# Copying A's rows 0 to 63 into T from SyncE's queue instead of ScalarE's, in a fused attention and feed-forward kernel

## The chip, the core and the metric

The kernel runs on one core of a Trainium2 chip. A core has five engines that run side by side, each in the order of its own instruction list: TensorE (PE) multiplies matrices, VectorE (DVE), ScalarE (ACT) and GpSimd (POOL) do elementwise work and reductions, and SyncE (SP) only issues DMAs. DMAs are issued from SyncE's queue or from ScalarE's. The metric is the device time of one execution in microseconds, the median of several runs.

## The reference

There are 4 batches of 8 heads with 768 positions of 64 features, and 16 centroids for each head.

```python
q_assign = argmax(q_n @ c_n.T); k_assign = argmax(k_n @ c_n.T)      # normalized q, k, centroids
scores = where(q_assign == k_assign, q @ k.T / 8, -1e9)
attn = exp(scores - max); attn = attn / (sum + 1e-9)
x = (attn @ v) with the heads side by side                            # 3072 x 512
h = x @ w_in                                                          # 512 -> 2048
out = (h * tanh(log1p(exp(h)))) @ w_out                               # 2048 -> 512
```

All inputs and the output are float32. Q and k of a head arrive stacked, 128 partitions by 768.

## The kernel before

**Precision.** Values are split into a high and a low part, and a product is made of three (high by high, high by low, low by high). For the scores of head n, A holds the high parts of q (partitions 0 to 63) and k (64 to 127), scaled; B holds the low parts. `prep_hi` on POOL makes A (lines 484 and 487), `prep_lo` on POOL makes B (line 500). T gets A's rows 0 to 63, Z gets B's rows 64 to 127, and then B's upper rows are overwritten from T and A's lower rows from A's upper rows: `copy_t`, `copy_z`, `copy_b`, `copy_a`. A cluster code (`hot_copy`) fills rows 64 to 79 of T and Z, so that one product adds the mask. The scores of a tile are two pairs of matmuls, B by A and T by Z (lines 631 and 636).

**Units.** The 32 heads n are cut into three units each of 256 query rows, 96 units i = 3n + qb, with two tiles a of 128 rows. The first 24 units (batch 0) run in float32: `rowmax` (VectorE), `expo` (ScalarE), transposes of p on TensorE, copies `pt` by ScalarE and VectorE, `pv`. Beside them the weights are loaded and split (`w_abs`, `w_low`, `w_f32`, `w_sq`, `w_hi`, `w_lo`; `w_lo` on VectorE is line 347). From unit 24 on, the probabilities are split into `hl` by `p_hi` (POOL, line 700) and `p_lo` (VectorE, line 717), and `ptrans` turns them by a DMA from SyncE's queue (`pt<-hl`, line 733). `pv` (line 753) multiplies a pair of units at once and needs all four transposes of the pair. `pv_out` (ScalarE) and `x_lo` (VectorE, line 814) make x; `m1`, `e_mish`, `e_gh`, `e_gl` and `m2` are the feed-forward part, which runs between the units of the next batch. A tail after the last unit uses seven products in place of eight.

**Order.** Every step has a due time in units of i, from the tables T and N, plus an entry of SHIFT for single steps. `Plan.run` issues the steps in the order of the due times, each after the steps that it needs, and ties the instructions of each engine to that order. So the tables fix the order on every engine and in every queue; the data set when an instruction can start. For n ≥ 9 the due time of a copy is 3n + N[kind]. A copy to T exists as a DMA for the 30 heads n ≥ 2; for the first two heads ScalarE copies.

**Queues.** `queue(n, kind)` chooses the issuing queue from T["dq", kind]: an integer other than 0 gives ScalarE, 0 gives SyncE. Before, `copy_t` has 3 and `copy_b` has −9 (both ScalarE); `copy_z` and `copy_a` have 0 (SyncE; most of `copy_a` is computed on ScalarE). The loads of qk, v and the weights, all transposes and the stores go out on SyncE's queue. T and Z have two buffers each, so the copy for n has to wait until the scores of n − 2 are done.

Of the kernel before, what the change touches and what calls it, by code (L numbers as in the profile page):

```python
# [72 lines left out]
def tile_clustered_attention_mish_ffn(  # L73
# [1211 lines left out]
    'v_sqd': -4.311,  # L1285
    'cent_put': -17.026,
    'ffn': 23.993,
    'w_f': 0.36,
    'w_q': 0.842,
    'w_lo': 0.312,  # L1290
    ('z', 'prep_hi'): -17.145,
    ('z', 'prep_lo'): -10.644,
    ('z', 'copy_t'): -21.55,
    ('z', 'copy_a'): -16.804,
    ('z', 'copy_b'): -16.943,
    ('z', 'copy_z'): -16.451,
# [31 lines left out]
    'copy_t': -0.79,  # L1328
    'prep_lo': -0.348,
    'prep_hi': 12.289,  # L1330
    'load': -4.71,
# [10 lines left out]
    ('dq', 'copy_t'): 3,  # L1342
# [25 lines left out]
    ('q_lo', 1): 6.955,  # L1368
# [25 lines left out]
    ('w_s', 1): -0.008,
# [41 lines left out]
    'pv': [4.606, 11.977, 4.089],
    'pv_out': 7.569,
    'x_lo': 2.785,
    'm1': [0.153, 0.664, 1.179, 1.534],
    'e_mish': [11.931, 1.622],  # L1440
    'e_gh': [2.313, 2.115],
    'e_gl': [1.659, 2.92],
# [10 lines left out]
    ('expo', 11, 0): -0.001, ('w_load', 10): -0.351, ('pv_out', 18): -0.443, ('scores', 24, 1): -0.221,  # L1453
    ('copy_b', 8): 0.081, ('scores', 25, 1): -1.54, ('w_lo', 2): 0.002, ('p_lo', 26, 1): 3.011,
    ('scores', 6, 0): -0.211, ('recip', 29, 0): 0.006, ('assign_mm', 0): 5.035, ('qk_load', 0): -4.812,
    ('qk_load', 1): 0.018, ('qk_load', 2): -7.858, ('qk_load', 3): 0.077, ('w_f32', 29): 3.258, ('w_low', 18): 0.746,
    ('w_low', 22): -0.606, ('pv', 5, 0): 0.121, ('w_low', 19): -0.124, ('pv_out', 10): 6.683,
# [12 lines left out]
    ('rowmax', 5, 0): 0.009, ('v_load', 1, 3): 0.118, ('w_load', 6): 0.644, ('copy_z', 0): -0.211,  # L1470
    ('prep_lo', 6): 5.99, ('copy_a', 6): -0.475, ('hot_copy', 0): 3.185, ('p_lo', 9, 1): 1.655,
    ('scores', 6, 1): 0.161, ('ptrans', 6, 0): 0.01, ('w_low', 4): 8.668, ('w_f32', 30): -0.084,
    ('w_f32', 28): -0.139, ('w_f32', 31): 0.04, ('copy_a', 7): 0.131, ('copy_a', 10): 0.5, ('p_hi', 13, 0): 1.089,
    ('p_hi', 14, 0): -3.366, ('p_hi', 15, 0): 0.165, ('p_hi', 16, 0): -3.157, ('p_hi', 16, 1): 0.035,
# [5 lines left out]
    ('copy_t', 0): 2.283, ('v_high', 0, 2): 1.174, ('assign_back', 2): -0.02, ('rowmax', 15, 0): -0.209,  # L1480
    ('x_lo', 16): 1.557, ('total', 19, 0): 0.011, ('assign_turn', 0): 0.477, ('hot_copy', 1): -0.189,
    ('pv_out', 12): 0.25, ('w_f32', 22): 0.284, ('pv_out', 23): 0.18, ('prep_lo', 9): -0.611, ('w_lo', 6): 0.291,
    ('x_lo', 27): 0.772, ('e_gh', 4): 1.076, ('assign_mm', 2): -0.078, ('hot_copy', 7): 0.903, ('hot_copy', 8): 0.259,
    ('p_lo', 14, 1): -0.992, ('p_lo', 2, 0): 0.919, ('scores', 0, 0): 2.293, ('expo', 3, 1): -0.54,
# [604 lines left out]
```

## Time and profile before

| what | us |
|---|---|
| median of 3 runs | 863.29 |
| lowest and highest | 861.83, 864.39 |
| the profiled execution, its own time | 866.38 |
| its span, first to last instruction | 864.6 |
| granted TensorE clock, mean | 1.0 |
| busy: TensorE, VectorE, ScalarE, POOL | 838.4, 690.2, 517.5, 431.4 |

The profile is of one execution. A busy time is the union of an engine's instructions; the issuing of DMAs is not counted as busy, and all of SyncE's work is of that kind. Matmuls are pipelined, so a busy TensorE is not one at its peak.

### The profile page before, as it was taken

Reading aid. Unit: us, or ns where it says so; the run is one execution under the profiler, and the core shown is the slowest. Engines: PE = TensorE matmul, PEld = TensorE weight load, DVE = VectorE, ACT = ScalarE, POOL = GpSimd, SP = SyncE. Lnnn points to the kernel's source line nnn. Section 1 sums busy time; section 2 is a strip of 40 time slices with the busy share of each in tenths; the row PEclk is TensorE's granted clock in tenths of the full one; section 3 lists DMA queues with packets and bytes.
Section 4 is the critical chain, followed back from the end, with each engine's and each line's share of the span. In section 5 each row is a group of like instructions: output and inputs, shape, how many; then the busy total and the mean of one; then the engine's idle time right before and its main releaser. Section 6 shows DMA issues by size and latency. Waiting matters only on the chain.

```text
span 864.6 us, 17394 instructions
## 1 busy us (share of the span) xinstructions
PE 838.4 (97%) x6671; PEld 613.0 (71%) x6671; DVE 690.2 (80%) x1178; ACT 517.5 (60%) x878; POOL 431.4 (50%) x410
## 2 busy tenths in 40 slices
PE   7999899989999999999999999999999999999998
PEld 3676676767777777776776766776777776777787
DVE  7989999898988798788877798777978876488831
ACT  6868878766565766565465765564564665245520
POOL 1464665686467446556576556465566543110000
PEclk9999999999999999999999999999999999999999
DMA  9865572398789987898889976988788876000000
GB/s 347 254 177 157 172 203 76 71 189 169 135 154 194 189 155 134 159 187 148 143 183 179 171 156 117 181 155 145 127 161 140 138 140 123 13 1 14 1 31 32
DMA packets 253060, 121.51 MB, mean 141 GB/s; under 512 B 230288, under 2 KB 230800, under 8 KB 252976
## 3 DMA queue, kind: packets, MB, share of 16 engines
q1 hardware_dynamic: 247632, 108.46, 60.7%
q10 hardware_dynamic: 5344, 11.93, 6.5%
q8 instruction: 53, 0.87, 0.5%
q14 instruction: 31, 0.25, 0.1%
HBM read 35.72 MB, written 6.29 MB: 49 GB/s over the span
## 4 chain that ended last, share of the span: by engine, by line
PE 73%; DVE 13%; DMA 6%; ACT 3%; issue 2%; POOL 2%; ACTq 0%; SPq 0%; DVEq 0%; POOLq 0%
PE o L753 9%; PE h L832 8%; PE h L834 8%; PE h L833 8%; PE O L873 7%; PE O L875 7%; PE O L874 7%; PE s L631 5%; PE s L636 5%; DVE m L648 4%; DMA pt<-hl 4%; DVE hl L717 2%; PE as L543 1%; DMA stage<-in_w_out_dram 1%; DVE w L347 1%
## 5 line engine op out<-in xcount | busy, mean ns | idle before, releaser
L662 ACT ACTIVATE p<-s,m 128x768 f32<-128x768 f32 x192 | 172.6, 899 | 159.4 <-DVE m L648 110.0
L700 POOL TENSOR_SCALAR hl<-p,l 128x768 f16<-128x768 f32 x144 | 167.4, 1165 | 171.9 <-DVE l L682 77.3
L648 DVE TENSOR_REDUCE m<-s 128x1 f32<-128x768 f32 x192 | 181.4, 950 | 26.7 <-PE s L636 24.5
L717 DVE SCALAR_TENSOR_TENSOR hl<-p,l,hl 128x768 f16<-128x768 f32 x144 | 172.2, 1200 | 11.8 <-POOL hl L700 11.3
L832 PE MATMUL h<-x,w 128*128 128x256 f16 x640 | 175.6, 274 | 1.4 <-DVE pt L729 0.7
L833 PE MATMUL h<-x,w 128*128 128x256 f16 x640 | 174.4, 273 | 0.0
L834 PE MATMUL h<-x,w 128*128 128x256 f16 x640 | 174.4, 273 | 0.0
L873 PE MATMUL O<-w,g 128*128 128x512 f16 x320 | 121.7, 380 | 0.0
L874 PE MATMUL O<-w,g 128*128 128x512 f16 x320 | 121.3, 379 | 0.0
L875 PE MATMUL O<-w,g 128*128 128x512 f16 x320 | 121.3, 379 | 0.0
L631 PE MATMUL s<-A,B 128*128 128x384 f32 x384 | 117.3, 386 | 2.6 <-ACT p L662 2.5
L849 POOL TENSOR_SCALAR g<-u,mscg 128x512 f16<-128x512 f32 x80 | 77.3, 969 | 66.3 <-ACT u L843 56.8
L857 DVE SCALAR_TENSOR_TENSOR g<-u,mscg,g 128x512 f16<-128x512 f32 x80 | 82.9, 1037 | 24.4 <-POOL g L849 24.2
L636 PE MATMUL s<-Z,T 80*128 80x384 f32 x384 | 99.2, 339 | 1.0 <-DVE T L603 1.0
L832 PEld LDWEIGHTS <-w 128*128 128x128 f16 x768 | 75.1, 98 | 28.6 <-issue 17.6
L753 PE MATMUL o<-pt,v 128*64 128x256 f16 x1296 | 79.4, 274 | 5.8 <-DMA pt<-hl 5.8
L833 PEld LDWEIGHTS <-w 128*128 128x128 f16 x768 | 75.5, 98 | 12.5 <-issue 1.5
L834 PEld LDWEIGHTS <-w 128*128 128x128 f16 x768 | 75.1, 98 | 8.7
L753 PEld LDWEIGHTS <-v 128*64 128x64 f16 x1296 | 68.6, 110 | 16.2 <-issue 9.9
L631 PEld LDWEIGHTS s<-A,B 128*128 128x128 f32 x384 | 62.2, 190 | 16.4 <-issue 4.6
L636 PEld LDWEIGHTS s<-Z,T 80*128 80x128 f32 x384 | 69.8, 189 | 1.3 <-ACT Z L600 1.3
L843 ACT ACTIVATE u<-h,msch 128x512 f32<-128x512 f32 x80 | 52.2, 686 | 29.0 <-PE h L834 21.9
(225 smaller groups left out, 1301.3 us busy)
## 6 DMA issues: line engine op xcount, KB each, us to landing
qk<-in_qk_dram SPq DMA_DIRECT2D x32, 384.0 KB, 4.7
stage<-in_w_in_dram SPq DMA_DIRECT2D x16, 512.0 KB, 7.4
stage<-in_w_out_dram SPq DMA_DIRECT2D x16, 512.0 KB, 4.5
vraw<-in_vP_dram SPq DMA_DIRECT2D x16, 384.0 KB, 5.7
T<-A ACTq DMA_DIRECT2D x30, 192.0 KB, 3.2
Z<-B SPq DMA_DIRECT2D x30, 192.0 KB, 3.4
B<-T ACTq DMA_DIRECT2D x28, 192.0 KB, 3.2
out_dram<-osb SPq DMA_DIRECT2D x20, 256.0 KB, 2.3
```

The lines of the kernel that those rows point to most:

```text
L631: nc.tensor.matmul(s[:, j, :384], st["B", n][:, q0 : q0 + P], st["A", n][:, j * 384 : (j + 1) * 384], start=True, stop=False,)
L636: nc.tensor.matmul(s[:, j, :384], st["T", n][: D + NCL, q0 : q0 + P], st["Z", n][: D + NCL, j * 384 : (j + 1) * 384], start=False, stop=True,)
L648: nc.vector.tensor_reduce(m, st["s", i, a][:, :, :384], axis=AX.XY, op=ALU.max, negate=True)
L662: nc.scalar.activation(p.rearrange("p (n x) -> p n x", n=2), st["s", i, a][:, :, :384], AF.Exp, bias=st["m", i, a], scale=1.0, accum_out=l,)
L717: nc.vector.scalar_tensor_tensor(t[:, 1], p, r, t[:, 0], op0=ALU.mult, op1=ALU.subtract)
L753: nc.tensor.matmul(o[s * D : s * D + D, :256], v if early else v[:, int(part == 1)], st["pt", 2 * m + s][:, :, c + (0 if early or part < 2 ...
L832: nc.tensor.matmul(o, wh, xh, start=(c == 0), stop=False)
L833: nc.tensor.matmul(o, wh, xl, start=False, stop=False)
L834: nc.tensor.matmul(o, wl, xh, start=False, stop=(c == 3))
L873: nc.tensor.matmul(o, gh, wh, start=(f == 0 and fi == 0), stop=False)
L874: nc.tensor.matmul(o, gh, wl, start=False, stop=False)
L875: nc.tensor.matmul(o, gl, wh, start=False, stop=(f == 7 and fi == 1))
```

## The change

The integer for `copy_t` in T becomes 0, so that its 30 DMAs go out on SyncE's queue. The function bodies stay as they are. The rest of the diff is new values in T, N and SHIFT: 54 of T's 129 entries, 37 of N's 48, and in SHIFT 1502 changed, 357 new and 4 dropped of 2524. Its core, with the entries that the prediction speaks of:

```diff
@@ T
-    ('dq', 'copy_t'): 3,
+    ('dq', 'copy_t'): 0,
-    'copy_t': -0.79,
+    'copy_t': -0.776,
-    'w_lo': 0.312,
+    'w_lo': 0.316,
...
@@ N
     'prep_hi': -3.459,
-    'copy_t': -2.7,
+    'copy_t': -3.354,
     'copy_z': -2.222,
-    'copy_a': -1.917,
+    'copy_a': -1.909,
...
@@ SHIFT
-    ('copy_t', 5): -0.446,
+    ('copy_t', 5): 0.094,
-    ('copy_t', 22): 0.405,
+    ('copy_t', 22): 1.078,
-    ('rowmax', 78, 1): 0.01,
+    ('rowmax', 78, 1): -0.277,
-    ('x_lo', 74): 0.255,
+    ('x_lo', 74): 0.338,
+    ('x_lo', 75): 0.968,
+    ('w_lo', 15): 3.882,
...
```

The due times of the single steps named below follow from these values and the formulas of the listing; `w_lo(15)`, for one, is due at N["ws"][15] + T["w_lo"] + SHIFT, 25.018 + 0.312 before and 24.953 + 0.316 + 3.882 now.

## Rows read from the trace of the kernel before

**Rows 1.** The page, part 1: busy time, share of the span, instructions.
```profile
PE 838.4 (97%) x6671; PEld 613.0 (71%) x6671; DVE 690.2 (80%) x1178; ACT 517.5 (60%) x878; POOL 431.4 (50%) x410
```

**Rows 2.** Windows: stretch, length, busy PE, PEld, DVE, ACT, POOL, clock, DMA, GB/s.
```profile
60.00:120.00 60.00, 54.78 (x434) 40.14 (x432) 57.72 (x97) 49.52 (x93) 32.67 (x39) 1.00 0.63 185
120.00:180.00 60.00, 54.84 (x421) 41.17 (x419) 53.33 (x101) 43.77 (x84) 40.79 (x41) 1.00 0.42 93
180.00:740.00 560.00, 553.90 (x4466) 401.39 (x4465) 457.24 (x758) 332.15 (x541) 327.48 (x286) 1.00 0.84 156
```

**Rows 3.** Waits of TensorE: total us, times, longest.
```profile
PE o L753 <- DMA pt<-hl: 5.8, 6, 1.6
```

**Rows 4.** Instructions on tile A: DMA issues, duration ns min/median/max.
```profile
L514 ACTq DMA_DIRECT2D T<-A x30: 468/468/518, 30.8 to 681.6; - x30
...
L514 SPq DMA_DIRECT2D A<-A x7: 494/536/1382, 74.8 to 673.7; - x7
```

**Rows 5.** The chain that ended last, 60 to 130 us: start, us, what.
```profile
88.54 0.47 ACTq L514
```

**Rows 6.** Timeline of TensorE, seven waits; the idle time before is in brackets.
```profile
89.58 1.08 PE L753 MATMUL o<-pt,vraw 128*64 128x256 f32 x6 [0.41 <-ACT pt L731]
...
111.44 0.76 PE L710 MATMUL q<-ident,p 128*128 128x128 f32 x5 [0.58 <-ACT p L662]
...
170.37 0.27 PE L832 MATMUL h<-x,w 128*128 128x256 f16 x1 [0.70 <-ACT u L843]
...
175.92 0.61 PE L631 MATMUL s<-A,B 128*128 128x384 f32 x2 [2.04 <-ACT p L662]
...
182.71 1.50 PE L753 MATMUL o<-pt,v 128*64 128x256 f16 x24 [0.96 <-DMA pt<-hl]
...
464.50 1.17 PE L753 MATMUL o<-pt,v 128*64 128x256 f16 x18 [1.38 <-DMA pt<-hl]
...
594.87 2.15 PE L753 MATMUL o<-pt,v 128*64 128x256 f16 x35 [1.62 <-DMA pt<-hl]
```

**Rows 7.** Timeline of ScalarE, two places.
```profile
108.91 0.47 ACTq L514 DMA_DIRECT2D T<-A  x1
...
461.10 0.47 ACTq L514 DMA_DIRECT2D T<-A  x1
```

**Rows 8.** DMA issues, 180 to 740 us: count, KB each, median us to landing.
```profile
Z<-B SPq DMA_DIRECT2D x22, 192.0 KB, 3.6
T<-A ACTq DMA_DIRECT2D x21, 192.0 KB, 3.3
...
pt<-hl SPq DMA_TRANSPOSE x140, 4.1
```

**Rows 9.** The chain before the pairs 60 and 76.
```profile
458.84 5.62 DMA pt<-hl
...
582.25 0.36 ACTq L514
...
583.75 0.42 DVE xx L814
...
587.74 0.87 DVE m L648
...
589.22 5.60 DMA pt<-hl
```

**Rows 10.** Timeline of SyncE, 455 to 470 us.
```profile
460.65 0.89 SPq L474 DMA_DIRECT2D qk<-in_qk_dram  x1
461.60 0.44 SPq L356 DMA_DIRECT2D vraw<-in_vP_dram  x1
```

**Rows 11.** Waits of SyncE's queue: total us, times, longest.
```profile
SPq L733 <- DVE hl L717: 133.4, 56, 5.3
```

**Rows 12.** Timeline of VectorE and of POOL at 167 us.
```profile
167.13 1.42 DVE L347 SCALAR_TENSOR_TENSOR w<-w,ws1r,w 128x1024 f16<-128x1024 f32 x1
...
167.46 1.87 POOL L700 TENSOR_SCALAR hl<-p,l 128x768 f16<-128x768 f32 x1
```

More of the change, by code (lines that the diff above doesn't have):

```diff
@@ L1427 @@
     'E': [0.384, 0.793, 1.234, 1.538],
-    'scores': 1.991,
+    'scores': 1.774,
     'rowmax': -0.3,
-    'expo': 3.904,
-    'total': 6.224,
+    'expo': 10.884,
+    'total': 6.302,
     'recip': 0.225,
-    'p_hi': 13.925,
-    'p_lo': 5.917,
+    'p_hi': 9.06,
+    'p_lo': 5.07,
     'ptrans': 0.818,
[L1436 to L1442, printed above, removed]
@@ L1449 @@
+    'm_out': 9.793,
+    'm_store': -0.442,
[3 rows of a table added]
 }
 SHIFT = {
[L1453 to L1457, printed above, removed]
@@ L1470 @@
[L1470 to L1474, printed above, removed]
@@ L1480 @@
[L1480 to L1484, printed above, removed]
@@ L1579 @@
-    ('p_hi', 24, 1): 0.826, ('p_hi', 25, 1): 0.716, ('p_lo', 28, 0): 0.229, ('p_lo', 28, 1): 2.539,
-    ('v_split', 0, 3): -0.06, ('v_split', 0, 1): -0.016, ('v_load', 1, 1): 0.317, ('ptrans', 19, 1): 0.105,
-    ('scores', 17, 1): 0.001, ('x_lo', 13): 0.266, ('p_hi', 9, 0): -0.021, ('pv_out', 19): 0.371,
-    ('pv_out', 17): 0.019, ('w_hi', 9): 4.053, ('w_low', 16): -0.221, ('w_lo', 3): 0.014, ('assign_hot', 2): 0.072,
-    ('rowmax', 22, 1): -0.123, ('expo', 15, 0): -0.084, ('qk_load', 7): 0.323, ('w_abs', 22): -0.017,
@@ L1584 @@
-    ('copy_a', 2): -1.413, ('m1', 6, 0): 1.422, ('e_gl', 1): -0.009, ('assign_back', 0): 2.408, ('w_abs', 20): -0.927,
-    ('pv_out', 8): 0.554, ('scores', 16, 0): 2.317, ('rowmax', 31, 0): -0.143, ('w_abs', 4): 0.104,
-    ('assign_max', 0): 1.285, ('hot_copy', 6): 0.017, ('assign_back', 1): 0.088, ('ptrans', 17, 1): -0.007,
-    ('expo', 6, 1): 1.076, ('x_lo', 29): -0.101, ('scores', 15, 0): 0.598, ('w_hi', 14): 0.913, ('copy_z', 8): 0.487,
-    ('p_lo', 17, 0): 0.344, ('scores', 1, 1): 3.429, ('rowmax', 19, 1): 0.01, ('w_sq', 16): 1.215,
@@ new lines @@
+    ('x_lo', 16): 1.557, ('total', 19, 0): 0.474, ('assign_turn', 0): 0.604, ('hot_copy', 1): -0.189,
+    ('pv_out', 12): 0.357, ('w_f32', 22): 0.369, ('pv_out', 23): 2.957, ('prep_lo', 9): -0.629, ('w_lo', 6): 0.291,
+    ('x_lo', 27): 0.592, ('e_gh', 4): 1.076, ('assign_mm', 2): 0.08, ('hot_copy', 7): 0.903, ('hot_copy', 8): 0.554,
+    ('p_lo', 14, 1): -0.992, ('p_lo', 2, 0): 1.367, ('scores', 0, 0): 2.293, ('expo', 3, 1): -0.54,
+    ('ptrans', 29, 0): 0.146, ('w_sum', 1): -0.11, ('assign_put', 2): 0.408, ('w_abs', 6): 0.161,
@@ new lines @@
+    ('w_load', 3): -0.316, ('rowmax', 26, 1): -0.136, ('total', 17, 1): -0.068, ('expo', 23, 0): -0.177,
+    ('w_lo', 10): -0.61, ('pv_out', 15): 0.265, ('assign_mm', 3): 3.259, ('p_lo', 12, 1): -0.197,
+    ('total', 20, 1): 1.896, ('e_gh', 2): -0.268, ('w_sq', 27): 3.267, ('w_sq', 6): 2.585, ('copy_b', 0): 0.86,
+    ('scores', 4, 0): 0.259, ('w_hi', 1): 0.386, ('hot_copy', 11): 0.649, ('prep_hi', 0): -0.295, ('w_load', 8): 2.33,
+    ('ptrans', 26, 1): -0.021, ('prep_hi', 3): -6.754, ('hot_copy', 3): -0.631, ('w_sq', 18): 0.052,
@@ new lines @@
+    ('scores', 25, 0): 0.563, ('scores', 26, 0): -0.169, ('ptrans', 24, 1): 0.073, ('ptrans', 25, 1): 0.037,
+    ('ptrans', 26, 0): 0.002, ('ptrans', 27, 0): -0.072, ('ptrans', 27, 1): -0.023, ('ptrans', 28, 1): -0.023,
+    ('ptrans', 29, 1): 0.054, ('prep_lo', 1): 0.695, ('x_lo', 22): 5.096, ('copy_z', 2): -0.303, ('w_load', 31): 0.66,
+    ('recip', 12, 1): 0.994, ('copy_a', 11): 0.022, ('total', 0, 0): 3.405, ('w_load', 2): -0.292,
+    ('total', 3, 1): 0.367, ('w_low', 20): 0.225, ('rowmax', 19, 0): 0.245, ('assign_stg', 0): -14.81,
@@ new lines @@
+    ('ptrans', 7, 1): 0.028, ('pv_out', 21): 1.094, ('p_lo', 27, 1): 1.452, ('recip', 26, 0): -0.024,
+    ('w_abs', 29): 0.05, ('total', 1, 0): -0.471, ('w_low', 0): 0.153, ('w_low', 2): -0.261, ('w_low', 7): 3.585,
+    ('w_low', 5): -0.999, ('w_low', 8): -1.486, ('w_low', 10): -0.254, ('copy_z', 11): 0.051, ('w_sq', 5): 0.304,
+    ('expo', 21, 0): -0.373, ('p_hi', 8, 1): -0.044, ('rowmax', 25, 1): 0.005, ('prep_hi', 11): 1.306,
+    ('m1', 2, 1): -0.458, ('hot_copy', 4): 4.62, ('w_abs', 12): -0.053, ('pv_out', 7): -0.005, ('w_sq', 3): 0.003,
@@ new lines @@
+    ('hot_copy', 6): 0.017, ('assign_back', 1): 0.105, ('ptrans', 17, 1): -0.15, ('expo', 6, 1): 0.969,
+    ('x_lo', 29): -0.101, ('scores', 15, 0): 0.569, ('w_hi', 14): 1.124, ('copy_z', 8): 0.487, ('p_lo', 17, 0): 0.344,
+    ('scores', 1, 1): 3.486, ('rowmax', 19, 1): 0.01, ('w_sq', 16): 1.215, ('w_abs', 14): -0.403,
+    ('recip', 4, 0): -1.418, ('expo', 5, 1): -0.85, ('w_lo', 0): -0.058, ('assign_put', 0): -2.449,
+    ('total', 0, 1): -0.188, ('total', 16, 1): 4.336, ('v_high', 0, 0): 3.268, ('scores', 10, 1): 0.05,
@@ new lines @@
+    ('x_lo', 5): 13.019, ('w_sq', 19): 6.549, ('qk_load', 8): -0.024, ('w_load', 1): 0.431, ('recip', 16, 1): 1.328,
+    ('expo', 12, 1): 2.798, ('x_lo', 14): -0.015, ('ptrans', 18, 0): -0.016, ('m1', 4, 1): -0.446, ('w_hi', 4): 0.039,
+    ('w_hi', 5): 0.02, ('w_hi', 6): 0.02, ('w_hi', 7): 0.068, ('recip', 3, 0): -0.434, ('scores', 8, 1): -0.056,
+    ('copy_t', 10): 0.093, ('ptrans', 18, 1): 0.228, ('w_lo', 8): 0.024, ('e_gh', 3): 0.119, ('e_gh', 5): 4.544,
+    ('scores', 16, 1): 1.306, ('expo', 9, 1): 0.648, ('w_abs', 7): -0.395, ('rowmax', 14, 0): 0.006,
@@ new lines @@
+    ('total', 23, 0): 0.334, ('assign_hot', 0): -3.792, ('copy_a', 1): 0.348, ('ptrans', 23, 0): -0.038,
+    ('scores', 5, 1): 0.342, ('p_lo', 19, 1): 5.202, ('p_hi', 12, 1): -0.065, ('cent_put',): -0.716,
+    ('ptrans', 16, 1): 0.006, ('w_f32', 27): -0.076, ('ptrans', 10, 1): 0.021, ('copy_z', 5): -0.143,
+    ('w_sum', 0): 0.553, ('qk_load', 6): 0.686, ('p_lo', 18, 1): 0.199, ('p_lo', 20, 0): -0.191,
+    ('p_lo', 21, 0): 1.382, ('scores', 22, 0): 4.36, ('ptrans', 2, 0): -0.017, ('x_lo', 18): 0.497,
@@ new lines @@
+    ('rowmax', 32, 0): 0.151, ('prep_hi', 17): 0.341, ('pv_out', 77): 0.367, ('pv', 14, 2): -0.364,
+    ('e_mish', 50): 1.79, ('recip', 78, 1): 0.067, ('rowmax', 65, 0): 0.145, ('scores', 56, 0): 0.154,
+    ('pv', 30, 1): 0.668, ('ptrans', 66, 1): -0.02, ('pv_out', 24): -2.309, ('pv_out', 25): -0.207,
+    ('pv', 35, 0): 2.031, ('x_lo', 19): 1.083, ('m_store', 2, 1): 0.156, ('m_store', 3, 0): 0.037,
+    ('p_lo', 46, 1): -0.028, ('p_lo', 47, 0): 2.572, ('p_lo', 47, 1): -1.201, ('p_lo', 48, 0): 1.054,
@@ L1879 @@
-    ('expo', 51, 1): 0.561, ('expo', 52, 1): 0.561, ('m1', 16, 0): -0.041, ('pv_out', 66): 0.781, ('x_lo', 65): 0.007,
-    ('e_mish', 6): 0.186, ('pv', 37, 0): 1.212, ('rowmax', 57, 1): -0.002, ('v_load', 2, 1): -4.014,
-    ('ptrans', 64, 0): 0.031, ('m1', 42, 0): 0.129, ('prep_hi', 19): 1.374, ('total', 49, 1): -0.327,
-    ('copy_a', 3): 0.197, ('scores', 12, 1): 1.219, ('ptrans', 63, 1): 0.154, ('x_lo', 23): -0.326,
-    ('expo', 30, 0): 0.594, ('rowmax', 77, 1): -0.265, ('p_hi', 55, 0): -0.459, ('p_lo', 55, 0): 1.045,
@@ new lines @@
+    ('scores', 57, 1): 0.771, ('rowmax', 81, 1): 0.044, ('prep_lo', 23): -0.342, ('hot_copy', 27): 0.462,
+    ('ptrans', 5, 0): 0.05, ('e_gh', 25): -0.32, ('total', 61, 1): 0.351, ('m1', 62, 1): 0.494,
+    ('expo', 11, 1): -0.038, ('recip', 80, 1): -0.02, ('copy_a', 15): 1.702, ('m2', 5, 1, 7): -0.139,
+    ('m_store', 0, 0): 0.017, ('copy_t', 11): 0.224, ('m1', 8, 0): -0.372, ('w_abs', 11): 0.036, ('x_lo', 0): 0.075,
+    ('x_lo', 2): 0.934, ('x_lo', 3): 0.057, ('w_lo', 4): 0.006, ('e_mish', 12): 2.395, ('p_hi', 67, 1): -0.057,
@@ new lines @@
+    ('m1', 16, 0): 0.096, ('pv_out', 66): 0.722, ('x_lo', 65): 0.007, ('e_mish', 6): -0.924, ('pv', 37, 0): 1.211,
+    ('rowmax', 57, 1): 0.355, ('v_load', 2, 1): -0.014, ('ptrans', 64, 0): 0.031, ('m1', 42, 0): 0.102,
+    ('prep_hi', 19): 1.374, ('total', 49, 1): -0.429, ('copy_a', 3): 0.197, ('scores', 12, 1): 1.229,
+    ('ptrans', 63, 1): 0.154, ('x_lo', 23): -0.326, ('expo', 30, 0): -0.971, ('rowmax', 77, 1): -0.182,
+    ('p_hi', 55, 0): -0.459, ('p_lo', 55, 0): 1.045, ('m2', 6, 1, 6): 0.007, ('m2', 2, 1, 3): 0.335,
@@ new lines @@
+    ('rowmax', 41, 1): 0.056, ('m_out', 3, 1): 2.005, ('m_out', 4, 0): 0.034, ('m_out', 4, 1): 2.266,
+    ('qk_load', 16): 0.128, ('ptrans', 70, 0): -0.087, ('p_lo', 80, 0): 0.302, ('recip', 87, 1): 5.215,
+    ('rowmax', 78, 1): -0.277, ('p_lo', 73, 0): -0.746, ('m2', 0, 0, 3): -0.054, ('ptrans', 33, 0): 0.136,
+    ('m2', 1, 1, 3): -0.856, ('recip', 62, 1): -0.003, ('e_mish', 53): 0.087, ('m1', 50, 0): 2.535,
+    ('x_lo', 76): -0.032, ('scores', 41, 0): 0.968, ('prep_lo', 14): 0.034, ('expo', 36, 0): 0.108,
@@ new lines @@
+    ('x_lo', 44): 0.456, ('v_split', 3, 2): 0.146, ('ptrans', 83, 0): 0.064, ('ptrans', 84, 0): -0.049,
+    ('ptrans', 84, 1): -0.049, ('ptrans', 85, 0): -0.1, ('ptrans', 85, 1): -0.049, ('ptrans', 86, 0): -0.049,
+    ('ptrans', 86, 1): -0.049, ('ptrans', 87, 0): -0.054, ('ptrans', 88, 1): -0.358, ('copy_t', 30): 0.482,
+    ('scores', 22, 1): 0.117, ('assign_put', 6): 0.319, ('m2', 4, 1, 3): -0.382, ('rowmax', 37, 1): 0.018,
+    ('e_gh', 19): 0.115, ('assign_back', 6): -0.946, ('p_lo', 63, 0): 0.555, ('recip', 76, 0): 0.115,
@@ new lines @@
+    ('assign_turn', 5): 0.198, ('rowmax', 14, 1): 0.032, ('m1', 53, 0): -0.034, ('ptrans', 3, 0): 0.03,
+    ('m1', 51, 1): -0.048, ('rowmax', 86, 1): -0.07, ('scores', 33, 0): 2.476, ('rowmax', 78, 0): 0.082,
+    ('copy_z', 30): -0.386, ('e_mish', 48): 1.688, ('e_mish', 54): -1.088, ('e_mish', 56): 0.082,
+    ('e_mish', 58): 0.063, ('e_mish', 59): 0.082, ('e_mish', 61): 0.082, ('e_mish', 65): 0.082, ('x_lo', 82): 0.162,
+    ('x_lo', 83): 0.155, ('x_lo', 84): 0.165, ('x_lo', 85): 0.489, ('x_lo', 86): 0.905, ('x_lo', 87): 0.155,
@@ new lines @@
+    ('pv', 34, 1): -4.676, ('pv', 35, 2): 1.847, ('pv', 36, 0): 0.016, ('pv', 37, 2): -0.351, ('pv', 39, 0): -0.168,
+    ('pv', 39, 2): 0.563, ('rowmax', 66, 0): -0.037, ('m2', 1, 0, 0): -0.463, ('ptrans', 69, 1): -0.157,
+    ('e_mish', 23): 0.073, ('p_lo', 83, 1): 0.62, ('assign_mm', 6): 0.109, ('scores', 9, 0): 4.218,
+    ('e_gl', 22): -0.1, ('ptrans', 59, 1): 0.278, ('ptrans', 4, 0): 0.02, ('rowmax', 85, 1): -0.021,
+    ('prep_hi', 27): -0.354, ('pv', 12, 1): -4.963, ('recip', 63, 0): -0.344, ('m2', 3, 0, 5): 0.044,
@@ new lines @@
+    ('expo', 32, 0): -1.983, ('m1', 39, 1): -0.038, ('copy_t', 15): 0.006, ('total', 78, 0): -0.57,
+    ('x_lo', 34): 0.037, ('x_lo', 35): 0.026, ('x_lo', 38): 0.026, ('x_lo', 40): 0.026, ('x_lo', 41): 0.026,
+    ('e_gl', 14): 0.081, ('rowmax', 36, 0): -0.197, ('pv_out', 5): 0.033, ('pv_out', 81): -0.183, ('e_gh', 11): -0.32,
+    ('ptrans', 69, 0): -0.287, ('m_out', 3, 0): 1.107, ('m1', 50, 1): 0.066, ('copy_a', 4): 0.03,
+    ('copy_z', 6): 0.385, ('v_high', 2, 0): 3.756, ('copy_b', 20): -0.053, ('w_lo', 14): 0.032, ('w_f32', 24): 0.019,
@@ new lines @@
+    ('m2', 5, 1, 2): -0.414, ('rowmax', 65, 1): 0.017, ('rowmax', 89, 0): 0.116, ('scores', 76, 1): 0.102,
+    ('x_lo', 50): 0.006, ('x_lo', 49): 0.285, ('assign_mm', 1): 0.192, ('prep_hi', 13): 0.046,
+    ('ptrans', 72, 0): -0.298, ('e_gh', 21): 0.146, ('e_gh', 23): 0.162, ('x_lo', 70): 0.139, ('p_hi', 57, 1): -0.086,
+    ('scores', 3, 0): 2.661, ('rowmax', 40, 1): 0.17, ('e_gl', 11): -0.303, ('m2', 7, 1, 0): -0.202,
+    ('x_lo', 77): -0.038, ('e_gl', 57): 0.008, ('ptrans', 77, 1): -0.069, ('ptrans', 78, 0): 0.042,
```

1259 lines of the change are left out of this document (642 added, 617 removed), and 56 rows, old and new, of tables (N, SHIFT).

## The prediction

> **What bounds the kernel now.** The page's busy times come first: TensorE (PE) is busy 838.4 us of the 864.6 us span [rows 1]. Its idle time is therefore some 26 us (864.6 − 838.4), and no change of order can give back much more than that. The windows by stage say where it lies [rows 2]. From 60 to 180 us, in the stage of the first 24 units, TensorE is idle 10.4 us (5.22 and 5.16), and VectorE (DVE) is busy 57.72 and 53.33 of 60 us: in that stage VectorE is as much the bound as TensorE. From 180 to 740 us TensorE is busy 553.90 of 560, so 6.1 us are left; ScalarE (ACT) is busy only 332.15 of these 560. The waits of TensorE name the reason for the late ones [rows 3]: `o` waits for the DMA `pt<-hl`, the transposed probabilities, 5.8 us in 6 waits, nearly all of the late idle time. The early waits are for ScalarE's `p` and `pt` and for VectorE's `w`. The granted clock is 1.00 in every window [rows 2], the 2.4 GHz level, so the clock plays no part.
>
> Nothing in this says that ScalarE or SyncE's queue is short of time on average. A gain must come out of single places where an engine that runs in order holds up the chain to one of those waits. So the parts are costed place by place.
>
> **Part 1, the copy leaves ScalarE's queue.** 30 copies of 0.468 us at the median [rows 4] free 14.0 us of ScalarE. Almost all of that is covered, because ScalarE is off the bound. Two early places are not. For n = 5 the chain runs through ScalarE's issue of the copy at 88.54, 0.47 us [rows 5]; the `pt` copy queued behind it ends a wait of 0.41 us of TensorE at 89.58 [rows 6]. For n = 6 the copy stands at 108.91 [rows 7], in front of an Exp that TensorE waits 0.58 us for at 111.44 [rows 6]. In both places ScalarE stood until POOL had A, and the issue came on top. With the copy gone the first stall can go whole (0.41) and the second by the issue time (0.47). Bounds: nothing, if VectorE, 96% busy here, is late in its place; 0.41 + 0.58 = 0.99 at the most. I take 0.88, near the upper end, because in both places what releases TensorE stands close behind the copy.
>
> **Part 2, late, the same copy beside the transposes.** From 180 to 740 us a transpose lands 4.1 us after its issue at the median [rows 8]. Two of the six stalls come with a copy to T in flight. Before the pair of units 60 and 61 the transpose issued at 458.84 takes 5.62 us [rows 9], and TensorE stands 1.38 us until 464.50 [rows 6]; ScalarE issued `T<-A` at 461.10 while it ran [rows 7]. By the due times in the diff the copy for n = 22 now stands behind `ptrans(62, 0)`, after this pair's transposes. The excess over the median is 5.62 − 4.1 = 1.52 us, and two more transfers started beside it, a qk load and a vraw load [rows 10], so I give T a third, 0.5 us. Bounds: 0 and the whole 1.38.
>
> Before the pair 76 and 77 the chain passes through the copy itself: its issue on ScalarE at 582.25, ScalarE's part of x behind it, VectorE's lower half of x at 583.75 (0.42 us), then the lower half of the probabilities, and at last the transpose at 589.22, which takes 5.60 us [rows 9]; TensorE stands 1.62 us until 594.87 [rows 6]. From 582.25 to 584.17 that is 1.92 us. In the new order `p_lo(77, 0)` goes ahead of both `x_lo(74)` and `x_lo(75)`, and the copy is gone, so it no longer waits for any of this. The pair's last `p_lo` still has `x_lo(74)` in front of it (0.42), and `rowmax(78, 1)` is put there too, 0.87 us by the like of it at 587.74 [rows 9]. With a share of 0.5 us for the flight of the transpose, as above, the gain is 1.92 − 0.42 − 0.87 + 0.5 = 1.1 us. Bounds: 0 and 1.62.
>
> The two shares of 0.5 us are the weakest terms: `T<-A` from ScalarE and `Z<-B` from SyncE, both 192 KB, land 3.3 and 3.6 us after issue [rows 8], so neither queue carries faster. The Trainium skill speaks against the shares: "DMA: Bandwidth & Descriptors", in "Issuing engines are not separate DMA queues", says that a DMA runs on the same 16 engines whoever issues it, and that the choice of issuer saves only the time its sequencer takes. By that rule the sum below would be 1.0 us smaller; the landing times just named agree with it.
>
> **Part 3, the copy joins SyncE's queue.** There it costs about 0.54 us of issue, the median of the seven `A<-A` copies of the same size that SyncE issues already [rows 4]: 16 us over 30 copies. Cover: SyncE's queue waits 133.4 us for VectorE's `hl` in front of transposes alone [rows 11]. Behind the copy stand transposes, loads and `copy_z`. The late due time goes from 3n − 2.70 to 3n − 3.354, while POOL's `prep_hi` stays at 3n − 3.459: the lead of A over its copy shrinks from 0.76 to 0.1 of a unit, and a unit lasts 560 / 72 = 7.8 us [rows 2]. So SyncE will at times stand at the copy until POOL has made A, and the transposes behind it start that much later. By the due times nearly all late copies stand just behind the last transpose of a pair (for n = 12, 16, 20 and 24 behind `ptrans(31, 1)`, `(43, 1)`, `(55, 1)` and `(67, 1)`), so the next transpose has a pair's time before it is needed. I take 0; bounds 0 and the second rival's price. A later T costs nothing as long as the scores of unit 3n are several microseconds away; if that cover is gone, TensorE waits for T itself.
>
> **Part 4, the rest of the order.** By the due times 665 of TensorE's 794 steps keep their place and most others move by one to three. The largest move that meets a stall is `w_lo(15)`: due at 29.15 in place of 25.33, from in front of `p_lo(24, 1)` to behind `p_lo(28, 0)`. In the trace it is VectorE's 1.42 us at 167.13, and POOL's `hl` beside it takes 1.87 us [rows 12]. The place is the tightest of the kernel: TensorE stands 0.70, 2.04 and 0.96 us until 170.37, 175.92 and 182.71 [rows 6], and this row of VectorE work leads to all three. Bounds: 0, if ScalarE's table load and Mish set the pace there, and 0.70 + 2.04 = 2.74. I take the instruction's own length, 1.4 us. In its new place I take 0, since VectorE waits for POOL and ScalarE there now and again. The other moves I take at 0 with 1.5 us either way: they are as many to the front as to the back.
>
> **The sum.** −0.88 (part 1) − 0.5 − 1.1 (part 2) − 1.4 (part 4) = −3.9 us. The profiled execution took 866.38 us (864.6 of span and 1.8 around it), which makes 862.5 for its like. It is 3.1 us above the median of the three runs shown, 863.29, so for a median the forecast is 863.29 − 3.9 = 859.4 us.
>
> **The rivals.**
> First, the stalls only change their place. VectorE's 57.72 of 60 us from 60 to 120 us [rows 2] means that what ScalarE gives back there is waited for at the next VectorE result, and T's bytes run beside the transposes from either queue. Then half of part 4 (0.7) and 0.4 of the chain at 582.25 stay: −1.1, 862.2 us. For it: TensorE's order is nearly the same. Against it: the stalls of part 1 end just behind the copy. This is also the case that the skill's sentence on issuers (same page and section as above) makes likelier.
>
> Second, slower: SyncE's queue becomes the wait. Six of the 36 late pairs have no slack [rows 3], and each microsecond by which their last transpose is late is TensorE's. If copies stand in front of these transposes, each costs 0.54 us of issue and about 0.5 us of flight: 6 × 1.04 = 6.2 us, less parts 1 and 4 (2.3), 867.2 us. It is slower than before from the point where three of the six are hit (3.1 − 2.3). Against it: the places read from the due times, and the 133.4 us of waiting.
>
> Third, more than forecast: the stalls of part 4 go whole (3.7 us with the 0.96), so do both of part 2 (3.0), and part 1's 0.99: −7.7, 855.6 us.
>
> **How the numbers follow.** A measurement of this kernel tells about 0.3% from no change, 2.6 us: faster means below 860.7, slower above 865.9. Chances: the forecast 0.38, more than forecast 0.14, stalls that move 0.32, slower 0.16. That gives faster 0.52, same 0.32, slower 0.16. The range runs from the third rival, 855.5, to the first with 1.5 us of other moves against it and the beginning of the second, 865.0.
>
> **What would show it.** Right: no `T<-A` on ScalarE; TensorE's idle time from 60 to 180 us down from 10.4 to about 8; the waits at 175.92 and 464.50 gone or below 1 us; SyncE waiting for POOL's A without a wait of TensorE behind it. Wrong: more than six waits of `o` for `pt<-hl`, or more than 5.8 us of them, or as much idle time from 60 to 180 us as before.

## The result, and the profile after

The changed kernel takes 874.13 us (median of 6 runs, 872.75 to 875.36), the kernel before 863.84 us beside it (6 runs, 861.83 to 865.83). The ratio is 1.0112, 95% interval 1.0093 to 1.0132: slower by about 9.7 us, where I had forecast 859.4 us and a range up to 865.0. The profiled execution of the changed kernel took 875.36 us, its span is 873.6 us.

First the page's busy times and the three windows that answer to [rows 1, 2]:

```profile
PE 843.9 (97%) x6671; PEld 616.3 (71%) x6671; DVE 697.6 (80%) x1178; ACT 519.4 (59%) x880; POOL 428.1 (49%) x410
```

```profile
60.00:120.00 60.00, 54.55 (x435) 39.66 (x435) 57.39 (x96) 49.62 (x93) 32.82 (x38) 1.00 0.66 184
120.00:180.00 60.00, 52.88 (x406) 40.55 (x406) 49.21 (x95) 42.51 (x83) 36.39 (x39) 0.97 0.37 89
180.00:740.00 560.00, 552.13 (x4398) 397.75 (x4397) 466.48 (x763) 334.15 (x543) 327.96 (x287) 1.00 0.84 155
```

The span is 9.0 us longer, and TensorE's busy time takes 5.5 of them (843.9 − 838.4), though it does the same 6671 matmuls. From 60 to 180 us TensorE is now idle 12.6 us (5.45 and 7.12) in place of 10.4; I had said about 8. The stage after 180 us is idle 7.9 us in place of 6.1. The granted clock is no longer 1.00 everywhere: it is 0.97 from 120 to 180 us, and 0.996 over the whole span. Of the 5.5 us of added busy time I put some 3.5 us down to that, an estimate: (1 − 0.996) × 873.6. It is not what makes the result, though: among the six runs are two at a clock of 1.000, and they took 872.94 and 874.58 us.

Three of TensorE's waits by cause (total us, times, longest). Before, the first was 5.8 us in 6 [rows 3], the third was not among the waits, and the second is shown ahead of the three:

```profile
PE s L631 <- ACT p L662: 2.5, 3, 2.0
```

```profile
PE o L753 <- DMA pt<-hl: 4.4, 8, 0.8
PE s L631 <- ACT p L662: 3.4, 5, 1.3
...
PE s L631 <- DMA B<-T: 2.4, 2, 2.1
```

And some of the places, in TensorE's timeline (the idle time before an instruction in brackets):

```profile
124.89 0.59 PE L631 MATMUL s<-A,B 128*128 128x384 f32 x2 [2.15 <-DMA B<-T]
...
174.07 0.27 PE L832 MATMUL h<-x,w 128*128 128x256 f16 x1 [1.41 <-ACT u L843]
...
179.59 0.62 PE L631 MATMUL s<-A,B 128*128 128x384 f32 x2 [1.31 <-ACT p L662]
...
212.28 2.15 PE L753 MATMUL o<-pt,v 128*64 128x256 f16 x35 [0.37 <-DMA pt<-hl]
...
234.54 2.15 PE L753 MATMUL o<-pt,v 128*64 128x256 f16 x35 [0.81 <-DMA pt<-hl]
...
357.12 0.62 PE L631 MATMUL s<-A,B 128*128 128x384 f32 x2 [0.86 <-ACT p L662]
```

What I had costed is partly seen: the waits of 1.38 us and 1.62 us of the two late pairs and the 0.96 us of the first late pair [rows 6] have no row of that size any more. But the waits at 174.07 and 179.59 are still 2.72 us (2.74 before, in the same two places), and there are new ones: for B's copy at 124.89, and small ones from 206 to 362 us, where before had only one of over 0.2 us, for `pt`, of 0.62 us at 259 us. Of the signs of being wrong that I had named, two came: eight waits for `pt` in place of six, and no less idle time from 60 to 180 us.

Last the copy itself, its issues (duration in ns min, median, max) and its flights from 180 to 740 us (count, KB, median us to landing), which answer to [rows 4, 8]:

```profile
L514 SPq DMA_DIRECT2D T<-A x30: 467/816/1497, 30.4 to 689.3; - x30
```

```profile
T<-A SPq DMA_DIRECT2D x22, 192.0 KB, 3.8
...
pt<-hl SPq DMA_TRANSPOSE x140, 4.0
```

An issue takes 0.82 us on SyncE at the median where I had taken 0.54. The transposes land as before, in 4.0 us (4.1), the copy in 3.8 us (3.3).

### The profile page after: what moved, and what is told of

Read it like the earlier page. It is cut to its first block, busy times and chain, and to the rows that moved or that the text cites. A ratio compares the mean times of both kernels' runs of the same rounds, so it can differ in the third digit from the quotient of the medians.

```text
span 873.6 us, 17388 instructions
## 1 busy us (share of the span) xinstructions
PE 843.9 (97%) x6671; PEld 616.3 (71%) x6671; DVE 697.6 (80%) x1178; ACT 519.4 (59%) x880; POOL 428.1 (49%) x410
## 5 line engine op out<-in xcount | busy, mean ns | idle before, releaser
L717 DVE SCALAR_TENSOR_TENSOR hl<-p,l,hl 128x768 f16<-128x768 f32 x144 | 177.5, 1237 | 12.8 <-POOL hl L700 12.2
```

Source lines behind the costliest of these rows:

```text
L717: nc.vector.scalar_tensor_tensor(t[:, 1], p, r, t[:, 0], op0=ALU.mult, op1=ALU.subtract)
```

## The experiments

Each run is timed in turns with the kernel before on the same chip. "Over before" is (ratio − 1) × 863.8 us. Where two runs are compared I take the difference of these. The expectations speak of an alignment of two traces: that is the start of the same matmul in both, one less the other.

| run | queue | order | us | ratio to before (95%) | over before |
|---|---|---|---|---|---|
| changed kernel | SyncE | new | 874.13 | 1.0112 (1.0093 to 1.0132) | +9.7 |
| e1 | SyncE | old | 875.84 | 1.0138 (1.0113 to 1.0163) | +11.9 |
| e2 | ScalarE | new | 886.66 | 1.0251 (1.0222 to 1.0279) | +21.7 |
| e3 | SyncE | new, w_lo(15) back | 874.02 | 1.0110 (1.0081 to 1.0138) | +9.5 |
| e4 | SyncE | old to unit 24, then new | 871.46 | 1.0090 (1.0065 to 1.0115) | +7.8 |
| e5 | SyncE | old, copy_t early | 862.98 | 0.9991 (0.9975 to 1.0007) | −0.8 |
| e6 | SyncE | old, copy_a late | 877.13 | 1.0139 (1.0113 to 1.0165) | +12.0 |
| e7 | SyncE | as e5 to unit 48, then new | 866.96 | 1.0039 (1.0025 to 1.0052) | +3.4 |
| e8 | SyncE | as e5, w_lo(15) moved | 863.10 | 0.9992 (0.9978 to 1.0007) | −0.7 |
| e9 | SyncE | as e5, 3 steps of GpSimd new | 863.34 | 0.9993 (0.9978 to 1.0007) | −0.6 |
| e10 | SyncE | as e5, 20 steps of VectorE new | 865.85 | 1.0015 (1.0002 to 1.0028) | +1.3 |
| e11 | SyncE | as e5, two copies back | 863.34 | 0.9987 (0.9972 to 1.0001) | −1.1 |
| e12 | ScalarE | as e5 | 875.18 | 1.0127 (1.0101 to 1.0154) | +11.0 |
| e13 | SyncE | new to unit 24, then as e5 | 867.17 | 1.0038 (1.0020 to 1.0056) | +3.3 |
| e14 | SyncE | new, 20 steps of VectorE back | 866.76 | 1.0036 (1.0020 to 1.0052) | +3.1 |

**The queue alone and the order alone.** Theory A was that the queue makes the loss, theory B that the new order does.

```diff
 e1, against the kernel before
-    ('dq', 'copy_t'): 3,
+    ('dq', 'copy_t'): 0,
 e2, against the changed kernel
-    ('dq', 'copy_t'): 0,
+    ('dq', 'copy_t'): 3,
```

> Before's order, and only the copy's queue changed from ScalarE to SyncE. Theory A (the queue makes the loss: a 3 to 5 us flight and SyncE's own queue of loads make the transposes and B's copies late): 870 us or more, ratio to before at least 1.007. Theory B (the new places in the order make the loss, the queue is harmless as I forecast): 862 to 866 us, ratio within 0.3% of 1, with the 1.38 us and 1.62 us stalls before the transposes of pairs 60 and 76 smaller.

> After's order with the copy left on ScalarE's queue. Theory A: within 0.4% of before, 860 to 867 us, and the 2.15 us wait of TensorE for B's copy at 122.8 us and the clock's fall behind it gone. Theory B: as the changed kernel, 872 to 876 us, and the waits of pairs 28 to 34 and of 330 to 364 us still there.

Neither theory holds: A's figure came in e1 and failed in e2, B's failed in both. Neither half by itself is faster than both together: the order alone is 12.0 us slower, the queue alone 2.2 us, which is within the intervals. The queue costs 11.9 us in the old order and gives back 12.0 us (21.7 − 9.7) in the new one, so its price depends on the order around it.

Where e1 loses its time is read from ScalarE's waits (total, times, longest), first before, then e1:

```profile
ACT A L512 <- DMA T<-A: 3.4, 2, 2.4
```

```profile
ACT A L512 <- DMA T<-A: 20.8, 7, 6.9
```

`copy_a` on ScalarE overwrites the rows that `copy_t` reads, so it waits until T has landed. The longest of the seven waits, in e1's timelines of SyncE, ScalarE and TensorE:

```profile
256.63 3.39 SPq L733 DMA_TRANSPOSE pt<-hl  x2
260.08 0.83 SPq L514 DMA_DIRECT2D T<-A  x1
```

```profile
264.54 0.83 ACT L512 CAST A<-A 64x768 fp32r<-64x768 f32 x1 [6.88 <-DMA T<-A]
```

```profile
266.44 0.62 PE L631 MATMUL s<-A,B 128*128 128x384 f32 x2 [0.77 <-ACT p L662]
...
268.43 0.27 PE L832 MATMUL h<-x,w 128*128 128x256 f16 x1 [1.03 <-ACT u L843]
...
271.72 1.01 PE L631 MATMUL s<-A,B 128*128 128x384 f32 x2 [0.92 <-ACT p L662]
```

In the old order the copy's turn on SyncE comes behind the next pair's transposes, which wait for VectorE's `hl`. GpSimd had this A ready at 246.14; the copy goes out at 260.08, lands 4.4 us later, ScalarE stands 6.88 us, and its Exps and Mish, all late, stop TensorE three times.

**The place of the copy.** Theory C was that this standing behind transposes is the whole price of the queue, theory D that the copy hurts on SyncE anywhere. Two ways to take the wait away:

```diff
 e5, against e1; so for each n from 9 to 31, at the changed kernel's due time
-    ('copy_t', 12): 0.462,
+    ('copy_t', 12): -0.753,
 e6, against e1; so for each n from 8 to 31, 0.65 later
-    ('copy_a', 12): 0.06,
+    ('copy_a', 12): 0.71,
```

> Before's order with the copy on SyncE (as in the queue-alone run), and one thing more: copy_t of heads 9 to 31 is due where the changed kernel has it, which puts it in SyncE's list ahead of the next pair's transposes, not between or behind them. Theory C (the queue costs because the copy stands behind transposes that wait for hl, T lands late, and ScalarE stands at copy_a, 20.8 us in 7 waits against 3.4 in 2): ScalarE's wait at copy_a below 6 us (the one for head 8 stays), 863 to 867 us. Theory D (the copy on SyncE hurts anywhere, by its issue time and its bytes in front of the transposes): 872 us or more.

> Before's order with the copy on SyncE, its place unchanged, but copy_a of heads 8 to 31 due 0.65 of a unit later, so that ScalarE reaches it after T has landed. Theory C: ScalarE's wait at copy_a falls below 6 us and the time comes back to 863 to 868 us. Theory D: as the queue-alone run, 874 to 878 us.

C holds in e5. The same copy now goes out ahead of the pair's transposes, ScalarE waits once at `copy_a`, and the time is that of the kernel before. From e5's timeline of SyncE and its waits:

```profile
247.06 0.51 SPq L514 DMA_DIRECT2D T<-A  x1
250.47 3.32 SPq L733 DMA_TRANSPOSE pt<-hl  x2
```

```profile
ACT A L512 <- DMA T<-A: 1.2, 1, 1.2
```

e6 missed: 877.13 us is what D forecast. Its wait for T fell from 20.8 us in seven to 5.6 us in one, as C expected, but that one is my own edit's: `copy_a(29)` is due ahead of its `copy_t` and pulls it, so with the one I moved the other, `copy_a` starts only at 650.30, and ScalarE's p behind it ends a wait of 4.54 us at 652.20. Up to the pair 78 the run bears C out in part: at the first matmul of that pair, e6 is 4.0 us behind before (618.66 against 614.68) and e1 11.7 us (626.42). As a whole e6 decides nothing.

The fourth combination was the early place on ScalarE's queue (e12 is e5 with 3 for `copy_t`), beside e11, which puts the copies of heads 14 and 15 back:

> The same early places of copy_t, but from ScalarE's queue. The changed kernel's order lost 12.5 us more on ScalarE's queue than on SyncE's (886.7 against 874.1). If that is because ScalarE stands at the early copy until GpSimd has made A and can't issue p: 867 to 876 us, with ScalarE waiting for GpSimd's A in front of p. If it was the rest of that order: within 2 us of before, 862 to 865.5 us.

> The run with copy_t early, but the copies of heads 14 and 15 at before's place. That run lost 1.3 us against before between 324 and 347 us (waits of 0.26 for stg and 0.59 for p), where the copy of head 15 goes out at 334 us. If the copy's place makes them: 861 to 862.5 us, and the two waits gone. If not, or if ScalarE then waits at copy_a: 863 us or more.

e12 is as slow as e1, from the other side. Its timelines of GpSimd, ScalarE and TensorE at the largest loss:

```profile
384.16 1.41 POOL L487 TENSOR_SCALAR A<-qk 128x768 fp32r<-128x768 f32 x1
```

```profile
385.60 0.48 ACTq L514 DMA_DIRECT2D T<-A  x1
386.19 0.90 ACT L662 ACTIVATE p<-s,m 128x768 f32<-128x768 f32 x1 [4.78 <-DVE m L648]
386.24 0.53 ACTq L514 DMA_DIRECT2D B<-T  x1
```

```profile
392.06 0.58 PE L631 MATMUL s<-A,B 128*128 128x384 f32 x2 [3.19 <-DMA B<-T]
```

GpSimd ends A at 385.57 (384.16 + 1.41) and ScalarE issues the copy at 385.60: it had stood for A. The profile puts the 4.78 us in front of p down to VectorE's m, but p is behind the copy in ScalarE's list, and the m that it needs had ended at 382.65. The older head's `B<-T`, also behind it, lands late, and TensorE stands 3.19 us. So: early on SyncE −0.8 us, early on ScalarE +11.0, late on ScalarE 0, late on SyncE +11.9. e11's 863.34 us falls on the side of "if not", but within the interval of e5; the two copies settle nothing.

**Where the new order loses.** With the copy early on SyncE, the new order was put in by stages.

```diff
 e4: tables T, N's u, w, ws and SHIFT of steps before unit 24 from the kernel before, the rest new
 e7: e5's order up to ('scores', 48, 0), then the new order
 e13: the new order up to ('scores', 24, 0), then e5's
```

> Copy on SyncE; the order of the early part (weights, pairs below 24, clusters below 9) as before, that of all that follows as after. By my alignment of the two traces 3.9 us of the loss arise before 180 us and some 5 us between 180 and 364 us, then 4 us are won and 5 lost again. If the losses stand where they arise and do not hang together: 868 to 872 us, without the 2.15 us wait at 122.8 us. If the early loss makes the later ones (everything behind it meets its loads at another time): 862 to 867 us.

> Before's order with copy_t early on SyncE up to the scores of unit 48, the changed kernel's order from there. If the new order loses between 180 and 364 us (4 to 5 us by the alignment) and wins 3 us at pairs 60 and 76: 861 to 865 us. If a new order of the late part is bad by itself: 868 us or more.

> The changed kernel's order up to the first scores of unit 24, from there the order of the run with copy_t early; the copy on SyncE throughout. If the parts of the loss add up: 862.98 + 2.7 = 865 to 866.5 us, with a wait for B's copy at 122 us. If the early part's loss is given back later (everything behind it only starts later into the same waits): 862 to 864 us.

Every stage costs. The early part costs 1.9 us (9.7 − 7.8, within the intervals) taken out of the changed kernel and 4.1 us (3.3 + 0.8) put into e5, a little more than I expected of e13. The part from unit 48 costs 4.2 us in e7 (3.4 + 0.8), between my two cases; one wait of 1.39 us of it, at the seam, is not in the changed kernel. The same part is worth 2 us more or less by what stands around it, so the parts can't simply be added.

The traces say where the loss arises. At the first matmul of a pair the changed kernel is behind e5 by 5.9 us at the pair 28, 9.5 at 34, 10.1 at 48 and 13.2 at the last pair, 94. Some 2 us of these are the two executions' own: the one profiled was 1.2 us above its median for the changed kernel and 0.8 below for e5.

**VectorE's steps in the middle.** `w_lo(15)` first, taken back in the changed kernel and moved alone in e5's order, then the other small moves of GpSimd and of VectorE between units 24 and 48:

```diff
 e3, against the changed kernel
-    ('w_lo', 15): 3.882,
 e8, against e5
+    ('w_lo', 15): 3.882,
 e9, against e5: prep_hi(11) two places later on GpSimd, v_high(0, 0) and (0, 1) two and six earlier
 e10, against e5: on VectorE w_lo(15) 38 places later, v_split(0, 1) 14 earlier,
   x_lo(32) 7, p_lo(35, 1) 4, x_lo(28) 4, p_lo(30, 1), p_lo(31, 0) 2 places later, 13 more by 2 to 5
 e14, against the changed kernel: the same 20 steps at their old places
```

> The changed kernel without the one entry that moves w_lo(15) behind the splits of pair 28. If w_lo(15) in its new place makes the loss of 208 to 260 us (pairs 28 to 34, 3.6 us): 870 to 872 us, those stalls gone, and stalls of up to 3.7 us at 170 to 183 us back in their place. If the move is worth what I forecast (1.4 us to the good, nothing in the new place): 874.5 to 876 us.

> As the run with copy_t early, and w_lo(15) moved as the change moves it. My fourth part says 1.4 us faster than that run (0 to 2.7). If the move is worth nothing, as putting it back in the changed kernel suggests (874.0 against 874.1 us): within 1 us of that run.

> The run with copy_t early (862.98 us) with three steps of GpSimd from the changed kernel's order of units 24 to 48: prep_hi(11) two places later, behind p_hi(28, 1) and an e_gh, and v_high(0, 0) and (0, 1) earlier. If GpSimd's order makes the waits of the pairs 28 to 34 in the changed kernel: waits for pt at 205 to 260 us that the base doesn't have, 0.4 to 2.5 us in all, 863.4 to 865.5 us. If not: within 0.5 us of the base, and no new wait there.

> The run with copy_t early with 20 steps of VectorE from the changed kernel's order of units 24 to 48 (six p_lo and x_lo steps two to seven places later, w_lo(15) 38 later, the v_split steps earlier, a few more). If VectorE's order makes the waits of pairs 28 to 34: 1 to 4.5 us of waits for pt there, 864 to 867.5 us. By my prediction's figure for other moves, 0 with 1.5 us either way: 861.5 to 864.5 us.

> The changed kernel with the 20 steps of VectorE between units 24 and 48 put back into before's places. If they are the cause of the waits at 208 to 266 us: 870 to 872 us (874.1 less 2 to 4), the pairs 28 to 34 without their waits of 0.3 to 0.8 us. If those waits come from elsewhere in the changed kernel: 873.5 us or more.

`w_lo(15)` shows no worth in either place (e3 and e8, 0.2 and 0.1 us; e3 lies between its two cases, and its interval is some 2.5 us either way), nor do GpSimd's three. VectorE's twenty are worth 2.1 us in e5's order (1.3 + 0.8) and 6.6 us in the changed kernel (9.7 − 3.1), more than I had expected and the largest single part of the loss. The traces agree on the place: from the pair 28 to the pair 34 the five profiles with nineteen or all of these moves fall behind e5 by 2.7 to 3.6 us (e4 2.7, e10 2.8, e3 3.5, e2 3.5, the changed kernel 3.6), and before, e7, e8, e9, e11, e12, e13 and e14 by 0.0. In e10 the same waits come up as in the changed kernel, at the pairs 28 and 32 and in the middle of 34. TensorE's waits for `pt` from 200 to 268 us, first in the changed kernel and, with the same figures, in e10, then in e14:

```profile
PE o L753 <- DMA pt<-hl: 1.4, 3, 0.8
```

```profile
PE o L753 <- DMA pt<-hl: 0.5, 1, 0.5
```

The profiles of before, e5, e7, e8, e9, e11 and e13, which have none of these moves (e8 has that of `w_lo(15)`), have one such wait there, of 0.4 to 0.7 us at 257 to 260 us. So these waits name 0.9 us of the 2.7 to 3.6; where the rest stands between the two pairs was not read.

What stands behind the longest of them, 0.81 us before the pair 32, is seen in the timelines of VectorE and SyncE ahead of that pair, first in e5, then in e10:

```profile
230.29 0.96 DVE L648 TENSOR_REDUCE m<-s 128x1 f32<-128x768 f32 x1
231.17 1.95 DVE L717 SCALAR_TENSOR_TENSOR hl<-p,l,hl 128x768 f16<-128x768 f32 x2
233.04 0.94 DVE L648 TENSOR_REDUCE m<-s 128x1 f32<-128x768 f32 x1
```

```profile
232.25 3.17 SPq L733 DMA_TRANSPOSE pt<-hl  x2
```

```profile
233.92 0.43 DVE L814 SCALAR_TENSOR_TENSOR x<-o,x 64x256 f16<-64x256 f32 x1 [0.18 <-ACT x L790]
234.38 1.82 DVE L648 TENSOR_REDUCE m<-s 128x1 f32<-128x768 f32 x2
236.12 1.94 DVE L717 SCALAR_TENSOR_TENSOR hl<-p,l,hl 128x768 f16<-128x768 f32 x2
```

```profile
237.19 4.98 SPq L733 DMA_TRANSPOSE pt<-hl  x2
```

In e5 one m stands ahead of the two `hl` of the pair and one behind them; in e10 both stand ahead. The `hl` end at 238.06 against 233.12 in e5, and the transposes start 4.9 us later. Of the 4.9 us, e10 is 3.3 us behind e5 already at the first matmul of the pair before (228.84 against 225.53), and 4.1 us at the x ahead of the m (233.92 against 229.84); the 0.9 us that come on top between this x and the `hl` are the length of one m.

## Why the prediction was wrong

**The step that failed is the last of part 4: "The other moves I take at 0 with 1.5 us either way: they are as many to the front as to the back."** With the copy early on SyncE the old order takes 862.98 us and the whole new order 874.13: the other moves cost 10.5 us (9.7 + 0.8). Here the moves did not cancel. In the one place read closely, an m put in front of a pair's last `hl` made the transposes later by its length, 0.9 us; that a step moved to the front gives nothing where the chain had slack is argued, not shown. Twenty moves of VectorE, most of two to five places, make 2.1 to 6.6 us of it, and the weight splits and early units some 2 to 4. From the pair 48 to the last, the five profiles with the new order there and the copy on SyncE (the changed kernel, e3, e4, e7, e14) fall behind e5 by 2.0 to 3.7 us, those with e5's order there (e8 to e11, e13) by −0.7 to 0.5; which moves do that was not tried. Why the twenty steps cost three times as much in the changed kernel as in e5's order stays open in part: from the pair 28 to the pair 48 the changed kernel falls 4.2 us behind e5 and e10 2.8, but e14, the new order without the twenty, gains 1.6. I had put VectorE beside TensorE as the bound of the early stage, where it is 96% busy, and behind it, where it is busy 82% (457.24 of 560 us), I priced its moves at nothing.

**The move of `w_lo(15)`, −1.4 us, was wrong.** The waits at 174 and 179 us are 2.72 us in place of 2.74, and e3 and e8 show no change of the time that could be measured. The case I named as the lower bound may hold, that ScalarE's table load and Mish set the pace there, since `u` and `p` end both waits; that is argued from the releasers, not tried.

**Part 3, the queue at 0, was right, but only in its place.** I had read that the late copies stand behind the last transpose of one pair, ahead of the next. In that place e5 measures −0.8 us for queue and place together (interval −2.2 to +0.6), with issues of 0.60 us at the median, not 0.54. In the place they had on ScalarE they cost 11.9 us (e1). My second rival had SyncE's queue as the slow mechanism, through transposes; in e1 the mechanism is the other way round, the transposes hold up the copy. In the changed kernel neither happens (ScalarE waits 1.5 us, once, at `copy_a`).

The Trainium skill, "DMA: Bandwidth & Descriptors", "Issuing engines are not separate DMA queues", says that another issuer saves only the sequencer's time. For the flights this case agrees: from 180 to 740 us the copy lands in 3.8 us from SyncE (e5) and 4.1 us from ScalarE (e12) in the early place, and in 3.4 us (e1) and 3.3 us (before) in the late one. For the time of the kernel it doesn't reach: the 12 us between the queues, in either sign, come from what an engine's own list puts in front of the issue and behind it.

**Part 1, −0.88 us, was wrong: the stalls moved.** In e5 the 0.41 us at 89.58 are gone, but the next wait for an Exp has grown from 0.24 to 0.64 us, and the 0.58 us at 111.44 are still 0.39. TensorE before, then in e5:

```profile
92.39 0.92 PE L710 MATMUL q<-ident,p 128*128 128x128 f32 x6 [0.24 <-ACT p L662]
```

```profile
90.87 0.92 PE L710 MATMUL q<-ident,p 128*128 128x128 f32 x6 [0.64 <-ACT p L662]
...
109.65 0.87 PE L710 MATMUL q<-ident,p 128*128 128x128 f32 x6 [0.39 <-ACT p L662]
```

At the same matmuls e5's trace gains 0.1 us over the first place and 0.2 over the second. In e1 and e7 to e11, with the same early order, the second wait is 0.56 to 0.59 us. For this part my first rival, stalls that only change their place, was right.

**Part 2 was right in kind.** In e5, with nothing but the copy changed, the waits before pairs 60 and 76 are gone and the trace gains 1.5 and 1.9 us there, where I had forecast 0.5 and 1.1. Its span is 4.2 us shorter than that of the profile before (860.4 against 864.6); 1.1 us of this arise before 60 us, where I had costed nothing. But the medians differ by 0.6 us only. The profiled execution before was 2.8 us above its median (866.38 against 863.55 in e5's comparison), e5's, at about 862.2 with the 1.8 around its span, some 0.8 below its own. So most of what I costed in part 2 from rows of that execution may be its own bad luck with transfers and not the kernel's; with one trace of before, this can't be told apart.

No version beats the kernel before by more than the measurement tells. e11 (0.9987) and e5 (0.9991) are the fastest, 11 us below the changed kernel, and both intervals reach 1.

## What to carry to other kernels

In a kernel laid out by hand, a DMA moved to another queue needs a new place in that queue's list: look for what it will stand behind there, what stands behind it, and which compute instruction waits for its landing. A queue and the order laid out for it are one thing: here neither half alone was faster than both together, and the order without its queue was 12 us slower. And many small moves in the order of an engine that is 80 to 96% busy were no noise around zero here; price those ahead of the last input of a tight chain one by one, and doubt gains read from a single execution that was slower than the median.

## What the runs showed of the hardware

After some waits of TensorE of 1.8 to 4.5 us the granted clock fell to half, the 1.2 GHz level, for a stretch. In the changed kernel's profile, two windows (columns as in [rows 2]): some 2 us after the 2.15 us wait that ends at 124.89, and later:

```profile
126.50:128.50 2.00, 2.00 (x10) 1.92 (x8) 1.83 (x8) 1.46 (x4) 1.94 (x2) 0.50 0.44 94
129.00:134.00 5.00, 5.00 (x38) 3.49 (x36) 3.16 (x6) 3.32 (x9) 3.88 (x4) 1.00 0.70 216
```

In that stretch a pair of the scores' matmuls takes 0.99 us in place of 0.59. The same happened behind the 1.79 us wait at 18.16 us, behind the 4.54 us wait of e6 (0.50 from 652 to 656 us), and in e1 around the three waits of 0.77 to 1.03 us at 266 to 272 us, where the clock from 262 to 275 us is 0.76. Such a stretch makes the matmuls themselves longer, so it shows as busy time of TensorE and not as a wait. It does not follow from the length of a wait alone: the wait of 2.04 us at 175.92 before [rows 6] left the clock at 1.00, and a wait of the same 2.04 us at 174.80 in e6 was followed by 0.50 from 176.5 to 179.5 us. Nor does it belong to an order of the kernel: behind the changed kernel's early order, the wait for B's copy that is 2.15 us in its profile is 0.82 us in e13, 0.54 in e3 and absent in e14, and none of these three profiles has the fall.
